# A hand-written order list for five engines, made longer and reordered at the start of a fused attention and channel-mix kernel

## The chip, the cores and the metric

The kernel runs on one core of one Trainium2 chip. The metric is the device time of one execution in microseconds (us); lower is better. Five engines take part: TensorE (PE, with its weight loads shown as PEld), VectorE (DVE), ScalarE (ACT), GpSimd (POOL), and SyncE (SP), which issues transfers.

## The reference

Two stages follow each other, in float32, for 4 sequences of 768 tokens and 512 features (8 heads of 64).

```python
for c in range(24):                       # chunks of 32 queries
    # keys: 8 memory rows and the window of up to 16 + 32 + 8 tokens around the chunk
    scores = 0.125 * q_c @ k_full.T
    a = exp(scores - max(scores)); a = a / (sum(a) + 1e-9)
    x[c] = a @ v_full
x_prev = x shifted by one token (zero in front)
xk = mu_k * x + (1 - mu_k) * x_prev
xr = mu_r * x + (1 - mu_r) * x_prev
k = maximum(xk @ w_k, 0)                  # 512 -> 1024
v = (k * k) @ w_v                         # 1024 -> 512
out = sigmoid(xr @ w_r) * v
```

## The kernel before

The 3072 tokens are dealt with in 12 units of 256 tokens, each of two tiles of 128. For unit u the work has these steps, and each is one named operation of a plan:

- `qk{t}` fetches the queries and keys of tile t, `vw{t}` its values. `s{u}` is the score product on PE (for unit 0 it is split: `s0` and `s0b`, one tile each). Then come `max{u}` and `sub{u}` on DVE, `exp{u}` on ACT, `sum{u}` on DVE, `norm{u}` on DVE or POOL.
- `t{t}` transposes the probabilities on PE (four products with the identity matrix `id`), `bd{t}.0` and `bd{t}.1` copy the two halves to SBUF on ACT or DVE, `a{t}` is the product with the values on PE, and `x{t}` copies the result out.
- For unit 0 alone the token shift is done on PE: `mix0.1` and `mix0.0` multiply the rows by two diagonal matrices, which `dg1` and `dg0` make from `id` and `mu` (lines 395 to 410). For later units `df{u}` and `mix{u}.m` do it on DVE. `xh{u}.m` and `xl{u}.m` split the result into a high and a low float32r part.
- `h{u}.n` is the product with w_k, `g{u}.n` that with w_r, `v{u}.n` that with w_v. Every one is made of three float32r products (high by high, high by low, low by high). `relu`, `sq`, `kh`, `kl` prepare the input of `v`; `sig` is the sigmoid, `o` the last multiplication, `out` the store.
- The weights come as ten loads of 1 MB, `w0.load` to `w9.load` (w0 and w1 are w_r, w2 to w5 are w_k, w6 to w9 are w_v). Each is decoded by `mag` (ACT), `low` and `join` (DVE), and split by `hi` and `lo`. `h0.0` needs w2 alone, `h0.1` w3, `h0.2` w4, `h0.3` w5. The `wz` operations form sums of w_v for a product scheme that later units use.

What decides the order is a planner (class `Plan`, lines 97 to 238). The list `FIRST` (lines 51 to 70) fixes order and engine of the first operations, up to `v0.3` in the kernel before; what is not in the list is placed greedily by due times, which `te_order` derives from `LEAD`. Every engine then works through its own instructions in that order. Transfers from HBM reuse four buffers named `big` (the `qk` and `w` loads), and a load waits until the buffer's last user is done.

Where the planner sees PE idle, the program adds "warm" products with a zero matrix (lines 1574 to 1580):

```python
n = 0 if ("ph", 0, 0) in T else int((o.start - busy - 0.1) / (0.86 if busy else 1.72))
```

Here `o.start` and `busy` are the planner's times, in which a `qk` load takes 1.68 of the transfer queue and lands 2.4 later, a `mu` load takes 0.1, a hop from engine to engine 0.17.

Of the kernel before, what the change touches and what calls it, by code (L numbers as in the profile page):

```python
# [50 lines left out]
FIRST = """
qk0@dma s0@pe qk1@dma max0@dve sub0@dve exp0@act s0b@pe max0b@dve mu@dma id@dma sum0@dve norm0@pool qk3@dma qk2@dma
w2.load@dma dg1@act vw0@dma vw1@dma w3.load@dma sub0b@dve exp0b@act sum0b@dve norm0b@dve dg0@act w2.mag@act s1@pe
t0@pe w4.load@dma bd0.0@act t1@pe w2.low@dve bd0.1@dve a0@pe w2.join@dve w2.hi@dve max1@dve sub1@dve qk5@dma
w2.lo@pool bd1.0@act bd1.1@act a1@pe qk4@dma x0@act x1@act mix0.0@pe mix0.1@pe w3.low@dve w3.mag@act w3.join@dve
vw2@dma exp1@act vw3@dma sum1@dve w5.load@dma w4.low@dve norm1@dve w4.mag@act w4.join@dve xh0.0@act w3.hi@act t2@pe
xl0.0@dve s2@pe xh0.1@act w4.hi@act bd2.0@act w0.load@dma bd2.1@dve w1.load@dma t3@pe bd3.1@act bd3.0@act a2@pe x2@act
xl0.1@dve w3.lo@dve qk6@dma a3@pe max2@dve h0.0@pe w4.lo@pool w5.mag@act w5.low@dve x3@act sub2@dve w5.join@dve
h0.1@pe h0.2@pe w0.low@dve vw4@dma exp2@act w0.mag@act sum2@dve w1.low@dve w5.hi@act w5.lo@dve h0.3@pe qk7@dma
w1.mag@act w0.join@dve w0.hi@act norm2@dve t4@pe w1.join@dve t5@pe w0.lo@dve relu0.1@act df1@dve relu0.0@act sq0.0@act  # L60
vw5@dma w1.hi@act bd5.1@act bd4.0@act w1.lo@dve sq0.1@act s3@pe g0.0@pe g0.1@pe relu0.2@act w7.load@dma mix1.1@dve
w6.load@dma mix1.0@dve bd4.1@act sq0.2@act kh0.1@act bd5.0@act xh1.1@dve xl1.1@dve w7.low@dve kl0.1@dve kh0.2@act
w8.load@dma xh1.0@act a4@pe xl1.0@dve kh0.0@act relu0.3@act kl0.0@dve w8.low@dve w7.mag@act w6.mag@act w9.load@dma
w7.join@dve w6.low@dve w6.join@dve sig0.0@act sig0.1@act a5@pe g1.0@pe g1.1@pe h1.0@pe sq0.3@act kh0.3@act h1.1@pe
kl0.3@pool x4@dve w7.hi@act x5@dve max3@dve sub3@dve sig1.0@act w7.lo@pool kl0.2@dve relu1.0@act sig1.1@act w6.hi@act
df2@dve w8.mag@act sq1.0@act w9.low@dve w6.lo@dve h1.2@pe h1.3@pe relu1.2@act relu1.1@act w9.mag@act relu1.3@act
sq1.2@act v0.0@pe w8.join@dve w9.join@dve sq1.3@act w8.hi@act mix2.1@dve v0.1@pe exp3@act w9.hi@act w8.lo@dve v0.2@pe
kh1.0@dve kl1.0@dve sq1.1@act w9.lo@dve kh1.1@act kl1.1@dve xh2.1@act xl2.1@dve mix2.0@dve kh1.2@act kl1.2@pool
v0.3@pe
"""  # L70
# [1560 lines left out]
```

## Time and profile before

| what | us |
|---|---|
| median of 3 runs | 390.93 (390.84 to 391.64) |
| the profiled execution | 391.39 |
| its span, first to last instruction | 389.6 |
| PE busy in the span | 381.5 |
| first product of mix0 starts | 19.30 |
| first product of g0.0 starts | 45.08 |

All times in the rows are microseconds from the start of the span, unless marked ns. A row of the timeline merges neighbouring instructions of one kind: start, length, engine, line of the kernel, operation, output and inputs, count, and in brackets how long the engine stood idle before it and what ended that.

### The profile page before, as it was taken

The page shows a single profiled execution, that of the slowest core. Times are in us where ns is not written, and L with a number is a line of the kernel's source. Part 1 is how long each engine was busy: PE and PEld are TensorE (multiplying, and loading weights), DVE is VectorE, ACT ScalarE, POOL GpSimd, SP SyncE. Part 2 cuts the span into 40 slices and gives each one's busy share as a digit, 9 for nine tenths or more (in the row PEclk, how much of TensorE's full clock was granted, in tenths as well). Part 3 has the DMA queues.
Part 4 walks back from the last instruction along what each step waited for, and adds up shares of the span by engine and source line. Part 5 has one row for each costly group of instructions (what it writes and reads, how often), then busy time and mean ns, then how long its engine had stood idle before and what let it go on. Part 6 is the DMA issues. An engine that isn't in the chain of part 4 may idle for free.

```text
span 389.6 us, 11005 instructions
## 1 busy us (share of the span) xinstructions
PE 381.5 (98%) x4736; PEld 351.8 (90%) x4736; DVE 324.2 (83%) x548; ACT 268.6 (69%) x455; POOL 16.0 (4%) x15
## 2 busy tenths in 40 slices
PE   8799999999999999999999999999999999999996
PEld 3589889888988999999999999999999899999996
DVE  3699999888898999969989989898999585976673
ACT  3877796914796789676588689877587746586631
POOL 2221004010000000000010000000000000000000
PEclk9999999999999999999999999999999999999999
DMA  8999870411053345435386576644046611133011
GB/s 314 414 374 368 324 301 2 141 56 54 2 204 116 130 154 183 153 128 216 116 309 211 193 272 207 216 175 144 2 163 190 203 56 42 32 132 109 0 56 54
DMA packets 25344, 63.43 MB, mean 163 GB/s; under 512 B 2512, under 2 KB 9040, under 8 KB 24784
## 3 DMA queue, kind: packets, MB, share of 16 engines
q1 hardware_dynamic: 25296, 62.73, 45.2%
q8 instruction: 37, 0.61, 0.7%
q14 instruction: 11, 0.09, 0.1%
HBM read 52.24 MB, written 10.49 MB: 161 GB/s over the span
## 4 chain that ended last, share of the span: by engine, by line
PE 92%; DMA 4%; ACT 2%; DVE 1%; SPq 0%; issue 0%
PE pr L1110 17%; PE ph L1134 15%; PE pc L1462 10%; PE pv L1110 9%; PE pa L1462 6%; PE B L1067 6%; PE pb L1462 6%; PE px L617 6%; PE G L1067 4%; PE A L1067 4%; PE s L520 4%; PE pt L600 2%; DMA vw<-in_vw_dram 2%; PE xf L671 2%; DMA wvl<-forms 1%; PE warm L1579 1%
## 5 line engine op out<-in xcount | busy, mean ns | idle before, releaser
L1134 PE MATMUL ph<-xh,wkh 128*128 128x256 f32 x192 | 53.5, 279 | 0.0
L1134 PE MATMUL ph<-xh,wkl 128*128 128x256 f32 x192 | 53.2, 277 | 0.1
L1134 PE MATMUL ph<-xl,wkh 128*128 128x256 f32 x192 | 53.1, 276 | 0.0
L1110 PE MATMUL pr<-wrh,xh 128*128 128x512 f32 x96 | 37.7, 393 | 0.0
L1110 PE MATMUL pr<-wrh,xl 128*128 128x512 f32 (+1 forms) x117 | 37.6, 351 | 0.0
L1110 PE MATMUL pr<-wrl,xh 128*128 128x512 f32 x96 | 37.5, 390 | 0.0
L1134 PEld LDWEIGHTS ph<-xh,wkl 128*128 128x128 f32 x192 | 36.0, 188 | 0.3 <-DVE wkl L448 0.3
L1134 PEld LDWEIGHTS ph<-xh,wkh 128*128 128x128 f32 x192 | 36.0, 188 | 0.3
L1409 DVE TENSOR_TENSOR khl<-k,khl 128x512 fp32r<-128x512 f32 x42 | 28.8, 688 | 8.8 <-ACT khl L375 8.3
L1134 PEld LDWEIGHTS ph<-xl,wkh 128*128 128x128 f32 x192 | 36.1, 188 | 0.0
L1110 PE MATMUL pv<-wvh,khl 128*128 128x512 f32 (+1 forms) x97 | 30.3, 390 | 0.0
L375 ACT CAST khl<-k 128x512 fp32r<-128x512 f32 x45 | 27.9, 621 | 2.6 <-PE pa L1462 1.5
L1462 PE MATMUL pc<-wtbig,khl 128*128 128x256 f32 x216 | 28.2, 280 | 0.0
L1462 PE MATMUL pa<-wvh,khl 128*128 128x256 f32 x144 | 28.2, 281 | 0.0
L375 ACT COPY aTz<-pt 64x512 f32<-64x512 f32 x43 | 24.8, 580 | 4.4 <-PE pt L600 3.6
L1462 PE MATMUL pb<-wtx,khl 128*128 128x256 f32 x216 | 27.5, 277 | 0.0
L617 PEld LDWEIGHTS px<-aTz,vw 128*64 128x64 f32 x768 | 23.5, 138 | 4.1 <-DVE aTz L377 2.3
L1229 ACT ACTIVATE k<-ph 128x512 f32<-128x512 f32 x23 | 13.5, 597 | 19.2 <-PE ph L1134 19.0
L617 PE MATMUL px<-aTz,vw 128*64 128x64 f32 x768 | 25.5, 224 | 1.2 <-DVE aTz L377 1.2
L1110 PEld LDWEIGHTS pr<-wrh,xl 128*128 128x128 f32 x117 | 22.0, 188 | 4.7
L1462 PEld LDWEIGHTS pc<-wtbig,khl 128*128 128x128 f32 x216 | 26.0, 188 | 0.1
L1462 PEld LDWEIGHTS pb<-wtx,khl 128*128 128x128 f32 x216 | 25.9, 188 | 0.0
(170 smaller groups left out, 1005.4 us busy)
## 6 DMA issues: line engine op xcount, KB each, us to landing
vw<-in_vw_dram SPq DMA_DIRECT2D x24, 512.0 KB, 5.0
ring<-in_qk_dram SPq DMA_DIRECT2D x16, 672.0 KB, 5.8
out_dram<-o SPq DMA_DIRECT2D x23, 256.0 KB, 2.2
qk<-in_qk_dram SPq DMA_DIRECT2D x8, 672.0 KB, 6.2
raw<-in_w_k_dram SPq DMA_DIRECT2D x4, 1024.0 KB, 7.7
raw<-in_w_v_dram SPq DMA_DIRECT2D x4, 1024.0 KB, 6.8
wvh<-forms SPq DMA_DIRECT2D x12, 256.0 KB, 3.4
wvl<-forms SPq DMA_DIRECT2D x12, 256.0 KB, 3.7
```

The lines of the kernel that those rows point to most:

```text
L375: e.copy(dst, src)
L520: nc.tensor.matmul(room(h, c)[CHUNK * j : CHUNK * (j + 1), r, :], q4[z, r, j, :], k3[z, r, STEP * j : STEP * j + NK], start=True, stop=True,)
L600: nc.tensor.transpose(p[:, n * P : (n + 1) * P], e[:, n // 2, c, n % 2, :], id_sb)
L617: nc.tensor.matmul(p3[64 * h : 64 * h + 64, 2 * g : 2 * g + 2, CHUNK * j : CHUNK * j + CHUNK], v[:, g, h, j, :], a[:, h, g, j, :], start=True,
L671: nc.tensor.matmul(z, T["diag", m][:, j, k], x[:, k, 1 - j : 1 - j + UTOK], start=j == 0, stop=j == 1)
L1067: nc.tensor.matmul(z, w, x[:, k], start=q in (1, 7) and i + k + m == 0, stop=i + k == 2 and m == 2, skip_group_check=q not in (1, 7),)
L1110: nc.tensor.matmul(p[:, a : a + step], x, w[:, a : a + step], start=start, stop=stop and a + step == DM)
L1134: nc.tensor.matmul(z, w, x[:, k], start=start, stop=stop)
L1229: e.activation(r, T["ph", u, f], AF.Relu)
L1409: nc.vector.tensor_sub(T["al", u, name], block(at), T["ah", u, name].bitcast(F32))
L1462: nc.tensor.matmul(p, l[:, i], r[i], start=start, stop=stop, skip_group_check=not fresh)
L1579: nc.tensor.matmul(warm, zero, zeros, start=True, stop=True)
```

## The change

The list is rewritten and goes on to `h2.3` and the first stores. VectorE makes the second diagonal matrix (`dg1`, two multiplications over 512 columns) in place of eight ScalarE activations; `1 - mu` becomes an operation of its own (`mu0`, `mu1`, ScalarE). The loads of `mu` and `id` are issued by ScalarE's queue and no longer by SyncE's. The warm products stop as soon as mix0 has begun, and no longer when h0 has begun.

```diff
-LEAD = """s0 t0 t1 a0 a1 mix0 mix1 h0.0 h0.1 s1 h0.2 h0.3 g0.0 g0.1 t2 t3 a2 a3
+LEAD = """s0 t0 t1 a0 a1 s1 mix0 mix1 h0.0 h0.1 h0.2 h0.3 g0.0 g0.1 t2 t3 a2 a3
...
-qk0@dma s0@pe qk1@dma max0@dve sub0@dve exp0@act s0b@pe max0b@dve mu@dma id@dma sum0@dve norm0@pool qk3@dma qk2@dma
-w2.load@dma dg1@act vw0@dma vw1@dma w3.load@dma sub0b@dve exp0b@act sum0b@dve norm0b@dve dg0@act w2.mag@act s1@pe
-t0@pe w4.load@dma bd0.0@act t1@pe w2.low@dve bd0.1@dve a0@pe w2.join@dve w2.hi@dve max1@dve sub1@dve qk5@dma
-w2.lo@pool bd1.0@act bd1.1@act a1@pe qk4@dma x0@act x1@act mix0.0@pe mix0.1@pe w3.low@dve w3.mag@act w3.join@dve
-vw2@dma exp1@act vw3@dma sum1@dve w5.load@dma w4.low@dve norm1@dve w4.mag@act w4.join@dve xh0.0@act w3.hi@act t2@pe
-xl0.0@dve s2@pe xh0.1@act w4.hi@act bd2.0@act w0.load@dma bd2.1@dve w1.load@dma t3@pe bd3.1@act bd3.0@act a2@pe x2@act
-xl0.1@dve w3.lo@dve qk6@dma a3@pe max2@dve h0.0@pe w4.lo@pool w5.mag@act w5.low@dve x3@act sub2@dve w5.join@dve
-h0.1@pe h0.2@pe w0.low@dve vw4@dma exp2@act w0.mag@act sum2@dve w1.low@dve w5.hi@act w5.lo@dve h0.3@pe qk7@dma
...
+qk0@dma s0@pe max0@dve mu@dma sub0@dve qk1@dma s0b@pe max0b@dve exp0@act qk2@dma sub0b@dve sum0@dve qk3@dma id@dma
+exp0b@act sum0b@dve norm0@dve w2.load@dma norm0b@pool mu1@act vw0@dma s1@pe max1@dve t0@pe mu0@act dg0@act bd0.0@act
+dg1@dve t1@pe vw1@dma w2.low@dve bd0.1@act bd1.0@act sub1@dve a0@pe x0@dve bd1.1@act w4.load@dma w2.mag@act w2.join@dve
+exp1@act w3.load@dma a1@pe sum1@dve w4.low@dve qk4@dma x1@act mix0.1@pe norm1@dve w2.hi@act qk5@dma w3.low@dve
+w4.mag@act w3.mag@act vw3@dma w4.join@dve w3.join@dve t2@pe mix0.0@pe bd2.0@act t3@pe xh0.1@act bd2.1@act w2.lo@dve
+vw2@dma w3.hi@act w3.lo@pool w5.load@dma xh0.0@act w4.hi@act bd3.0@act w5.mag@act xl0.1@dve bd3.1@act s2@pe xl0.0@dve
+w0.load@dma max2@dve w4.lo@pool sub2@dve a2@pe w0.mag@act w5.low@dve h0.0@pe w0.low@dve x2@act w5.join@dve exp2@act
+qk7@dma w1.load@dma a3@pe qk6@dma w0.join@dve sum2@dve w5.hi@act h0.1@pe w7.load@dma w0.hi@act w5.lo@dve w1.mag@act
+w1.low@dve h0.2@pe x3@act vw4@dma w1.join@dve w1.hi@act h0.3@pe s3@pe w9.load@dma norm2@dve t4@pe relu0.2@act w1.lo@dve
+w0.lo@dve df1@dve sq0.2@act t5@pe mix1.1@dve mix1.0@dve w9.low@dve relu0.0@act sq0.0@act relu0.3@act w6.load@dma
+vw5@dma xh1.0@dve w6.low@dve relu0.1@act bd5.1@act xl1.0@dve g0.0@pe bd4.0@act w7.mag@act bd5.0@act bd4.1@act
+w6.mag@act g0.1@pe kh0.0@act a4@pe w7.low@dve w8.load@dma w9.mag@act w6.join@dve sq0.3@pool max3@dve w8.low@dve
...
-    o_id = op("id", ("dma", 0.2), lambda: nc.sync.dma_start(id_sb, ident))
-    o_mu = op("mu", ("dma", 0.1), lambda: nc.sync.dma_start(mu_sb[:, 0:2], mu))
+    o_id = op("id", ("dma", 0.2), lambda: nc.scalar.dma_start(id_sb, ident))
+    o_mu = op("mu", ("dma", 0.1), lambda: nc.scalar.dma_start(mu_sb[:, 0:2], mu))
...
-            nc.scalar.activation(mu_sb[:, 2 + m], mu_sb[:, m], AF.Copy, scale=-1.0, bias=1.0)
             for j in range(2):
+                if m == 1:
+                    nc.vector.tensor_mul(
+                        T["diag", m][:, j],
+                        id_sb.unsqueeze(1).to_broadcast([P, KT, P]),
+                        mu_sb[:, m + 2 * j].unsqueeze(2).to_broadcast([P, KT, P]),
+                    )
+                    continue
...
-        diag[m] = (op(f"dg{m}", ("act", 2.0), f, [o_id, o_mu], new=d), d)
+        def f_rest():
+            nc.scalar.activation(mu_sb[:, 2 + m], mu_sb[:, m], AF.Copy, scale=-1.0, bias=1.0)
+
+        o = op(f"mu{m}", ("act", 0.2), f_rest, [o_mu])
+        diag[m] = (op(f"dg{m}", ("dve", 1.35, True) if m else ("act", 2.45), f, [o_id, o], new=d), d)
...
-                n = 0 if ("ph", 0, 0) in T else int((o.start - busy - 0.1) / (0.86 if busy else 1.72))
+                n = 0 if ("xf", 0, 0, 0) in T or ("xf", 0, 1, 0) in T else int((o.start - busy - 0.1) / (0.86 if busy else 1.72))
```

## Rows read from the trace of the kernel before

**Rows 1.** The page's first part: busy time of each engine, share of the span.

```profile
PE 381.5 (98%) x4736; PEld 351.8 (90%) x4736; DVE 324.2 (83%) x548; ACT 268.6 (69%) x455; POOL 16.0 (4%) x15
```

**Rows 2.** Timeline of PE, from s0b to the first mix0.

```profile
6.50 0.86 PE L520 MATMUL s<-qk 64*32 64x64 f32 x64 [0.69 <-DMA qk<-in_qk_dram]
7.29 2.84 PE L1579 MATMUL warm<-zero_sb 128*128 128x512 f32 x6
10.41 1.06 PE L520 MATMUL s<-qk 64*32 64x64 f32 x85 [0.28 <-DMA qk<-in_qk_dram]
12.62 0.68 PE L520 MATMUL s<-qk 64*32 64x64 f32 x43 [1.14 <-issue]
13.23 1.09 PE L600 MATMUL pt<-id_sb,e 128*128 128x128 f32 x8
...
16.00 2.09 PE L617 MATMUL px<-aTz,vw 128*64 128x64 f32 x64 [0.82 <-DVE aTz L377]
18.02 1.12 PE L1579 MATMUL warm<-zero_sb 128*128 128x512 f32 x2
19.30 7.14 PE L671 MATMUL xf<-xTs,k 128*128 128x256 f32 x32 [0.15 <-PE warm L1579]
```

**Rows 3.** The chain that ended last: start, length, what.

```profile
45.15 5.67 PE pr L1110 x25
...
386.41 0.42 DVE o L1501
```

**Rows 4.** Waits of PE over the span: total, times, longest.

```profile
PE px L617 <- DVE aTz L377: 1.2, 2, 0.8
```

**Rows 5.** The page's groups: busy, mean ns, idle before, releaser.

```profile
L1134 PEld LDWEIGHTS ph<-xh,wkl 128*128 128x128 f32 x192 | 36.0, 188 | 0.3 <-DVE wkl L448 0.3
```

**Rows 6.** Transfers issued from 10 to 11 us: instruction queue (packets, MB, share).

```profile
q8 instruction: 1, 0.02, 5.9%
```

**Rows 7.** Timeline of DVE up to 60 us.

```profile
12.46 0.69 DVE L559 TENSOR_TENSOR e<-e,sm_sb 128x512 f32<-128x512 f32 x1
...
26.84 1.28 DVE L685 TENSOR_TENSOR xl<-xf,xh 128x512 fp32r<-128x512 f32 x2
...
32.03 1.22 DVE L535 TENSOR_REDUCE sm_sb<-s 128x16 f32<-128x1024 f32 x1
33.18 0.68 DVE L438 TENSOR_SCALAR raw<-raw 128x1024 uint32<-128x1024 uint32 x1
33.77 1.22 DVE L544 TENSOR_TENSOR e<-s,sm_sb 128x1024 f32<-128x1024 f32 x1
34.91 1.22 DVE L442 SCALAR_TENSOR_TENSOR mag<-mag,raw 128x1024 uint32<-128x1024 uint32 x1
...
36.64 1.22 DVE L553 TENSOR_REDUCE sm_sb<-e 128x16 f32<-128x1024 f32 x1
...
38.27 0.64 DVE L438 TENSOR_SCALAR raw<-raw 128x1024 uint32<-128x1024 uint32 x1
...
58.05 2.22 DVE L442 SCALAR_TENSOR_TENSOR mag<-mag,raw 128x1024 uint32<-128x1024 uint32 x1
```

**Rows 8.** Timeline of ACT up to 22 us.

```profile
7.67 0.63 ACT L548 ACTIVATE e<-e 128x512 f32<-128x512 f32 x1 [5.65 <-DVE e L544]
...
11.26 2.43 ACT L405 ACTIVATE k<-id_sb,mu_sb 128x128 f32<-128x128 f32 x8
13.60 1.16 ACT L435 ACTIVATE xx<-raw 128x1024 f32<-128x1024 f32 x1
14.65 1.65 ACT L375 COPY aTz<-pt 64x512 f32<-64x512 f32 x3
...
20.58 1.06 ACT L548 ACTIVATE e<-e 128x1024 f32<-128x1024 f32 x1 [0.80 <-DVE e L544]
21.54 1.16 ACT L435 ACTIVATE mag<-raw 128x1024 f32<-128x1024 f32 x1
```

**Rows 9.** Transfers issued before 10 us: count, KB, us to landing.

```profile
id_sb<-in_ident_dram SPq DMA_DIRECT2D x1, 64.0 KB, 4.7
```

More of the change, by code (lines that the diff above doesn't have):

```diff
@@ L57 @@
-xl0.0@dve s2@pe xh0.1@act w4.hi@act bd2.0@act w0.load@dma bd2.1@dve w1.load@dma t3@pe bd3.1@act bd3.0@act a2@pe x2@act
-xl0.1@dve w3.lo@dve qk6@dma a3@pe max2@dve h0.0@pe w4.lo@pool w5.mag@act w5.low@dve x3@act sub2@dve w5.join@dve
-h0.1@pe h0.2@pe w0.low@dve vw4@dma exp2@act w0.mag@act sum2@dve w1.low@dve w5.hi@act w5.lo@dve h0.3@pe qk7@dma
-w1.mag@act w0.join@dve w0.hi@act norm2@dve t4@pe w1.join@dve t5@pe w0.lo@dve relu0.1@act df1@dve relu0.0@act sq0.0@act
-vw5@dma w1.hi@act bd5.1@act bd4.0@act w1.lo@dve sq0.1@act s3@pe g0.0@pe g0.1@pe relu0.2@act w7.load@dma mix1.1@dve
@@ L62 @@
[L62 to L66, printed above, removed]
@@ L67 @@
-sq1.2@act v0.0@pe w8.join@dve w9.join@dve sq1.3@act w8.hi@act mix2.1@dve v0.1@pe exp3@act w9.hi@act w8.lo@dve v0.2@pe
-kh1.0@dve kl1.0@dve sq1.1@act w9.lo@dve kh1.1@act kl1.1@dve xh2.1@act xl2.1@dve mix2.0@dve kh1.2@act kl1.2@pool
-v0.3@pe
+qk0@dma s0@pe max0@dve mu@dma sub0@dve qk1@dma s0b@pe max0b@dve exp0@act qk2@dma sub0b@dve sum0@dve qk3@dma id@dma
+exp0b@act sum0b@dve norm0@dve w2.load@dma norm0b@pool mu1@act vw0@dma s1@pe max1@dve t0@pe mu0@act dg0@act bd0.0@act
+dg1@dve t1@pe vw1@dma w2.low@dve bd0.1@act bd1.0@act sub1@dve a0@pe x0@dve bd1.1@act w4.load@dma w2.mag@act w2.join@dve
@@ new lines @@
+w1.low@dve h0.2@pe x3@act vw4@dma w1.join@dve w1.hi@act h0.3@pe s3@pe w9.load@dma norm2@dve t4@pe relu0.2@act w1.lo@dve
+w0.lo@dve df1@dve sq0.2@act t5@pe mix1.1@dve mix1.0@dve w9.low@dve relu0.0@act sq0.0@act relu0.3@act w6.load@dma
+vw5@dma xh1.0@dve w6.low@dve relu0.1@act bd5.1@act xl1.0@dve g0.0@pe bd4.0@act w7.mag@act bd5.0@act bd4.1@act
+w6.mag@act g0.1@pe kh0.0@act a4@pe w7.low@dve w8.load@dma w9.mag@act w6.join@dve sq0.3@pool max3@dve w8.low@dve
+xh1.1@act kh0.2@act kl0.0@dve xl1.1@dve kl0.2@dve w6.hi@act kh0.3@act w9.join@dve w8.mag@act w8.join@dve sq0.1@dve
@@ new lines @@
+a5@pe h1.0@pe relu1.0@act sig0.0@act w8.hi@act h1.1@pe w6.lo@dve w9.hi@act vw7@dma h1.2@pe qk8@dma sig0.1@act g1.0@pe
+wz0.01@dve w8.lo@dve w7.join@dve sq1.0@act kh0.1@act wz0.11@dve sig1.0@act wz0.t3@dve x4@act relu1.2@act kl0.1@dve
+w7.hi@act w9.lo@dve kl0.3@dve wz0.h3@act wz0.l3@dve h1.3@pe wz0.00@dve g1.1@pe w7.lo@pool x5@act sub3@dve relu1.1@act
+df2@dve v0.0@pe wz0.t1@dve sq1.2@act mix2.1@dve exp3@act v0.1@pe v0.2@pe v0.3@pe mix2.0@dve xh2.1@act wz0.10@dve
+relu1.3@act xh2.0@act wz0.t2@dve wz0.t4@dve xl2.0@dve wz0.h2@act wz0.l2@dve wz0.h1@act wz0.l1@dve h2.0@pe wz0.h4@act
@@ new lines @@
+wz0.l4@dve wz1.01@dve wz1.11@dve sig1.1@act xl2.1@dve wz1.t3@dve kh1.0@act wz1.h3@act sq1.1@act qk9@dma g2.0@pe
+sum3@dve o0.0@dve wz1.l3@dve g2.1@pe wz1.00@dve vw6@dma sq1.3@act o0.1@dve kh1.3@act kl1.0@dve kl1.3@dve wz1.t1@dve
+kh1.1@dve kl1.1@dve h2.1@pe wz1.h1@dve sig2.0@act kh1.2@dve wz1.t2@dve relu2.0@act wz1.h2@dve wz1.10@dve out0.0@dma
+wz1.t4@dve v1.0@pe kl1.2@pool wz1.l1@dve wz1.l2@dve sq2.0@act wz1.h4@dve norm3@dve v1.1@pe wz1.l4@dve sig2.1@act
+wz2.01@dve v1.2@pe wz2.11@dve wz2.t3@dve relu2.1@dve wz2.h3@dve sq2.1@dve wz2.l3@dve o1.0@dve v1.3@pe wz2.00@dve
@@ L70 @@
+wz2.t1@dve kh2.1@dve wz2.t2@dve h2.2@pe wz2.h1@dve kh2.0@dve out0.1@dma wz2.10@dve h2.3@pe wz2.t4@dve o1.1@dve
+out1.1@dma kl2.0@pool out1.0@dma
 """
```

## The prediction, made before the changed kernel ran

> **What bounds the kernel now.** The page's busy line comes first: PE 381.5 us of a 389.6 us span [rows 1]. The chain that ended last says where the rest is. It is PE from one end to the other, apart from the first 19 us, and closes with one DVE multiplication at 386.41 and its store [rows 3]. So only three things can move the time: when PE's unbroken work begins, the few holes in it, and what follows its last product. The change touches nothing of the last. PE's own list of waits is short: the attention product waits twice, 1.2 us in all [rows 4], of which 0.82 lie before mix0 [rows 2] and 0.4 before the next one. The page's group of h0's weight loads adds 0.3 us behind a DVE `lo` [rows 5].
>
> Now the timeline of PE. The first long work, mix0, starts at 19.30, and from there to g0.0 at 45.15 [rows 2, 3] PE needs 25.85 us, in which it stood for 0.4 (a2) and 0.3 (h0.3): 25.15 us without holes. After 45.15 the waits list has next to nothing left. The price of the whole change is thus read from two numbers, the start of mix0 and the holes up to g0.0. Before 19.30 PE holds little work, so what counts there is the chain of others: t0 and t1 at 13.23, ACT occupied by dg0 until 13.7 and by w2.mag until 14.65, only then the copies bd, a0 at 16.00, the x copies, and one superfluous pair of warm products that ends at 19.14 [rows 2, 8].
>
> The least obvious row is the one at 12.62. s1 stops after 85 of its 128 products and goes on 1.14 us later, with the cause "issue" [rows 2], that is nothing the profile shows. Just before, from 10 to 11 us, the instruction queue moved a packet of 0.02 MB [rows 6]. I read the hole as PE waiting for its next block of instructions.
>
> **The change part by part.**
>
> *Start to s1.* mu, now ahead of qk1 in the planner's order, moves the planned start of s0b by 0.1, so the gap that the warm formula sees grows from 0.81 to 0.91 and passes 0.86: one warm pair is put between s0 and s0b, and one fewer stands before s1. A pair is 2 of the 6 products of 2.84 us, 0.95 us, and s0b now starts at 6.50 after 0.69 us of idleness [rows 2], so it starts near 6.8, 0.3 us later. If the block of instructions is asked for while s0b runs, it too comes up to 0.3 us later. Bounds for the end of s1: 13.3 as before, 13.9 if the block is held up by twice that; I take 13.6, between them, since only one delay is in sight. As many instructions stand ahead of the hole as before, so by my reading it stays and the sum is the one below; if its cause were the time of a transfer, it could go, and the sum would be that of the first rival. Beside this: the Trainium skill, Runtime: NRT & Kernel Launch, § Terms, says that an engine's instruction memory is refilled in blocks of 16 KiB, so that a hole would be tied to a count of instructions. The packet's 0.02 MB agrees; no row names the engine that it served. The time that SP saves on mu and id brings qk2 and qk3 forward, but s1 runs into the hole anyway: worth nothing.
>
> *dg1 to VectorE, and what queues behind.* ACT loses eight activations, 2.43 us [rows 8], DVE gets two multiplications over 512 columns; the nearest row is the half norm, 0.69 [rows 7]. From below it is 0.6 each (overlapped, as the 0.68 `low` gives way after 0.59), from above 0.7: I take 1.3 for both. It isn't hidden: behind s1 DVE has max1, dg1, w2.low, sub1 in this order, ACT then exp1 and behind it x1, and mix0.1 waits for x1. From row starts: max1 1.15, dg1 1.3, low 0.6, sub1 its full 1.22, exp1 0.96 until the next ACT instruction starts, x1 0.59 (a 512-column copy like bd, 0.55 to 0.6) [rows 7, 8], and some 0.13 of hops. 13.6 + 1.15 + 1.3 + 0.6 + 1.22 + 0.96 + 0.59 + 0.13 = 19.55. The values don't bind: ACT, with dg0 (2.43) started after exp0b near 10, is free for bd0.0 when t0 is done near 14.2, four copies at 0.55 end by 16.4, and a0 and a1 are done by 17.5, before w2.mag and sub1 let exp1 begin at 17.9. So mix0 begins 0.25 us later than at present, between 19.2 and 19.9 with the bounds.
>
> *mix0 to g0.0.* PE's own work is the same 25.15 us if nothing is late. The check, from starts of rows [rows 7]: `low` 0.6, `sub` 1.14 (33.77 to 34.91) and so `join`, `lo` and `norm`, whose rows have the same length, `sum` 1.63 (36.64 to 38.27), two-part `xl` 1.28. norm1 ends 17.85 + x0 0.7 + 1.14 + 1.63 + 0.6 + 1.21 = 23.1, and t2 may start at 19.55 + 3.57 = 23.12: no slack. xl0.0, seven steps on, ends at 29.7, h0.0 is due at 30.2. w5.lo ends near 38.5, h0.3 is due at 39.5. In all DVE has 28 operations, 30 us, from max1 to w0.lo: 13.6 + 30.2 = 43.8, and g0.0 is due at 44.7. So the two old holes, 0.4 and 0.3, go: the second since w5.lo no longer stands behind w1.low, which waits for its load. w2.lo moves from POOL to DVE and w3.lo the other way, which cancels; w2.hi, bd0.1 and bd2.1 go to ACT (some 2.1 us less for DVE) and pay for dg1 and x0.
>
> *Rest of the list, LEAD and the condition on warm products.* No warm row stands behind 18.02 among those before h0, so the new condition removes none. The rest reorders a stretch in which PE had no hole; I cost it at nothing, under cover of PE's own work, and bound it by 0.3 of new waits (as rows 5) and 0 gain.
>
> Sum: mix0 +0.25, holes -0.7, 19.55 + 25.15 = 44.7 against 45.15: 0.45 us less. With the bounds of mix0 that is 0.1 to 0.8 less. The profiled execution took 391.39 (its span and 1.8 around it) and would take 390.9; the median of the runs lies 0.46 lower, so I say 390.5.
>
> **The rivals.** *The hole in s1 goes or ends early.* Then DVE goes from norm0 straight into max1. norm0 is done near 12.1, an estimate: the half norm at the end of the same chain ends at 13.15 now [rows 7], behind an exp0b that stood behind eight activations of 2.43 us on ACT [rows 8], and I take 1.1 of these off. max1 follows at once, and mix0 starts at 12.1 + 5.95 (the steps above) = 18.05: 19.3 - 18.05 and the 0.7 of holes make 1.95 us, 389.0. For it: the cause is inferred. Against: the count of instructions is equal.
>
> *DVE falls behind.* At t2 and at h0.0 the slack is 0 to 0.5, so each microsecond lost on DVE there is paid. The price is that of one `join` of 2.22 against 1.22 [rows 7], which ran beside POOL work: 1.0, which turns -0.45 into +0.55, 391.5. The list keeps POOL's work beside DVE's reads of PSUM, which speaks against it.
>
> *id comes late (slower).* On ScalarE's queue its load stands behind exp0 (7.67 to 8.30 now [rows 8]). If it is issued only then, and takes 0.8 to issue and 4.7 to land as now [rows 9], it lands at 13.8; dg0 ends at 16.2, four bd at 18.4, w2.mag 19.5, exp1 20.5, x1 21.1: mix0 at 21.1 and g0.0 at 46.3, 1.1 us slower, 392.0. It decides from a landing at 12.3 on, and is a loss from 12.7. Against it: nothing makes the transfer itself wait. Beside this: the Trainium skill, Perfetto Trace Analysis, § on DVE and Act instructions, has an engine's instruction wait in a queue of its own while the sequencer reads on; by that id goes out right after mu and the rival falls. No row here shows a transfer issued by ScalarE.
>
> **How the numbers follow.** A measurement of this kernel tells 0.2% (0.8 us) from no change. Forecast 0.48, of which 0.12 lies at its fast end beyond 0.8; no or short hole 0.25; small gains later 0.05 (faster); DVE behind 0.12 (same, or a little slower by 0.02); id late 0.10. Faster 0.42, same 0.46, slower 0.12. Range: from a little under the hole's absence, 388.8, to DVE behind, 391.5; outside lie the late id and a little at the fast end. The forecast's own range is 390.1 to 390.8.
>
> **What would show it.** Right: s1's second part near 12.9, dg1 on DVE between max1 and w2.low, x1 directly behind exp1 near 18.9, mix0.1 at 19.2 to 19.9, no wait at t2 or a2, g0.0 about 25.2 after mix0.1, the rest as before. Wrong: s1 without its hole; dg0 starting after 12; t2 or h0.0 waiting for DVE; new PE waits behind 45; a granted clock below 1.

## The result, and the profile of the changed kernel

The change made the kernel slower: 396.49 us (median of 6 runs, 395.73 to 397.27) against 390.91 (6 runs, 390.75 to 392.58), a ratio of 1.0134, 95% interval 1.0111 to 1.0157. The forecast was 390.5. The profiled execution took 397.19, 5.80 more than that of before.

First the two numbers to which the forecast had reduced everything, the start of mix0 and what follows it. In the timeline of PE of the changed kernel (`warm` are the filling products, `pt` belongs to t0 and t1, `px` to a0 and a1, `xf` to mix0):

```profile
5.44 1.18 PE L537 MATMUL s<-qk 64*32 64x64 f32 x64 [0.59 <-DMA qk<-in_qk_dram]
6.55 1.13 PE L1596 MATMUL warm<-zero_sb 128*128 128x512 f32 x2
7.61 0.86 PE L537 MATMUL s<-qk 64*32 64x64 f32 x64
8.39 1.98 PE L1596 MATMUL warm<-zero_sb 128*128 128x512 f32 x4
10.31 1.07 PE L537 MATMUL s<-qk 64*32 64x64 f32 x85
14.53 0.92 PE L537 MATMUL s<-qk 64*32 64x64 f32 x43 [3.16 <-issue]
15.60 1.94 PE L617 MATMUL pt<-id_sb,e 128*128 128x128 f32 x8
19.06 3.69 PE L634 MATMUL px<-aTz,vw 128*64 128x64 f32 x64 [1.52 <-ACT aTz L382]
22.68 1.58 PE L1596 MATMUL warm<-zero_sb 128*128 128x512 f32 x2
24.36 3.69 PE L688 MATMUL xf<-xTs,k 128*128 128x256 f32 x16
```

mix0 starts at 24.36 instead of 19.30 [rows 2], 5.06 us later. From there to the end of the span it is 395.4 - 24.36 = 371.0 us against 389.6 - 19.30 = 370.3 before. So 5.06 of the 5.8 us are lost ahead of mix0 and 0.7 behind it. Ahead of it, three things differ from rows 2. The hole in s1 (the stretch with the cause "issue") is 3.16 us long instead of 1.14. a0 starts 3.06 later. And the products of a0 and a1 need 3.69 for what took 2.09.

The timeline of ACT says why a0 is late (`ACTq` is ACT's queue issuing a transfer):

```profile
0.75 0.40 ACTq L399 DMA_DIRECT2D mu_sb<-in_mu_dram  x1
1.18 1.28 ACT L565 ACT_TABLE_LOAD   x1 [1.18 <-PEq L1636]
8.48 0.63 ACT L565 ACTIVATE e<-e 128x512 f32<-128x512 f32 x1 [6.02 <-DVE e L561]
8.49 0.36 ACTq L398 DMA_DIRECT2D id_sb<-in_ident_dram  x1
...
15.49 2.45 ACT L418 ACTIVATE k<-id_sb,mu_sb 128x128 f32<-128x128 f32 x8 [4.73 <-DMA id_sb<-in_ident_dram]
17.84 1.77 ACT L382 COPY aTz<-pt 64x512 f32<-64x512 f32 x3
```

mu goes out at once. id does not: its issue appears at 8.49, 0.01 behind the start of exp0, which stands ahead of it on ACT and waits for DVE until 8.48. Then the transfer takes 7.0 us to land, where SyncE's took 4.7 [rows 9]:

```profile
id_sb<-in_ident_dram ACTq DMA_DIRECT2D x1, 64.0 KB, 7.0
```

ACT stands idle for 4.73 us, dg0 starts at 15.49, and bd0.0, on which a0 waits, is queued behind dg0 on ACT. The chain of work that ended last runs through this load and not through s1 (start, length, what; the longest pieces):

```profile
8.49 6.97 DMA id_sb<-in_ident_dram
19.06 3.70 PE px L634 x64
24.36 3.69 PE xf L688 x16
```

Why a0 and a1 are slow shows in the windows (per stretch: span, busy time and instructions of PE, PEld, DVE, ACT, POOL, granted clock, DMA share, GB/s), first of the changed kernel, then of before:

```profile
10.00:13.00 3.00, 1.38 (x86) 0.91 (x85) 2.35 (x7) 0.76 (x3) 0.89 (x1) 1.00 0.99 406
13.39:23.63 10.24, 7.43 (x116) 6.25 (x117) 6.71 (x8) 7.68 (x17) 0.00 (x1) 0.50 0.79 322
23.63:30.00 6.37, 6.27 (x30) 5.01 (x29) 6.30 (x9) 4.22 (x6) 0.00 (x0) 1.00 0.88 304
```

```profile
13.39:23.63 10.24, 9.26 (x96) 7.06 (x96) 8.73 (x9) 8.37 (x15) 2.37 (x1) 1.00 1.02 413
```

From 13.39 to 23.63 TensorE was granted half its clock, 1.2 GHz of 2.4. The fall came in s1's hole, 2.0 us after its last product and 2.1 us before id landed. In the kernel before, the clock was whole throughout the span.

### The profile page after: what moved, and what is told of

Its sections match the earlier page's. It is cut to its first block, busy times and chain, and to the rows that moved or that the text cites. A ratio compares the mean times of both kernels' runs of the same rounds, so it can differ in the third digit from the quotient of the medians.

```text
span 395.4 us, 11007 instructions
## 1 busy us (share of the span) xinstructions
PE 384.8 (97%) x4734; PEld 354.8 (90%) x4734; DVE 327.0 (83%) x556; ACT 264.9 (67%) x441; POOL 16.5 (4%) x16
## 4 chain that ended last, share of the span: by engine, by line
PE 91%; DMA 6%; ACT 1%; DVE 1%; SPq 0%; issue 0%
PE ph L1151 17%; PE pr L1127 15%; PE pc L1479 10%; PE pv L1127 8%; PE px L634 6%; PE pa L1479 6%; PE B L1084 6%; PE pb L1479 6%; PE G L1084 4%; PE A L1084 4%; PE s L537 4%; PE pt L617 2%; DMA vw<-in_vw_dram 2%; PE xf L688 2%; DMA id_sb<-in_ident_dram 2%; DMA wvl<-forms 1%
## 5 line engine op out<-in xcount | busy, mean ns | idle before, releaser
L382 ACT COPY aTz<-pt 64x512 f32<-64x512 f32 x46 | 26.7, 580 | 6.1 <-PE pt L617 5.3
L634 PE MATMUL px<-aTz,vw 128*64 128x64 f32 x768 | 27.5, 232 | 2.2 <-ACT aTz L382 1.5
L634 PEld LDWEIGHTS px<-aTz,vw 128*64 128x64 f32 x768 | 25.2, 145 | 4.7 <-ACT aTz L382 1.9
L382 ACT CAST khl<-k 128x512 fp32r<-128x512 f32 x41 | 25.4, 622 | 2.0 <-PE pa L1479 0.9
L1198 ACT ACTIVATE sg<-pr 128x512 f32<-128x512 f32 x24 | 14.4, 599 | 17.4 <-PE pr L1127 15.8
```

The costliest lines, as they stand in the source:

```text
L382: e.copy(dst, src)
L634: nc.tensor.matmul(p3[64 * h : 64 * h + 64, 2 * g : 2 * g + 2, CHUNK * j : CHUNK * j + CHUNK], v[:, g, h, j, :], a[:, h, g, j, :], start=True,
L1198: nc.scalar.activation(T["sg", u][:, c * DM : (c + 1) * DM], T["pr", u, c], AF.Sigmoid)
```

## The experiments

All times of rows come from each kernel's profiled execution. "Rest" is its span less the start of mix0, so it grows by every wait and every slower product behind mix0. Two kernels ran once only and have no ratio. Each ratio compares with runs of before made beside that kernel's own; their medians lie between 390.91 and 391.94.

| kernel | median us | ratio to before, 95% | id lands | s1 resumes | mix0 | rest |
|---|---|---|---|---|---|---|
| before | 390.91 | | 6.8 | 12.62 | 19.30 | 370.3 |
| after | 396.49 | 1.0134 (1.0111 to 1.0157) | 15.5 | 14.53 | 24.36 | 371.0 |
| E1 after, both loads on SyncE | 394.90 | 1.0087 (1.0058 to 1.0115) | 11.3 | 13.67 | 20.30 | 371.8 |
| E2 after, id ahead of exp0 | 394.88 | 1.0081 (1.0065 to 1.0097) | 7.3 | 13.68 | 20.32 | 372.2 |
| E3 before, both loads on ScalarE | 399.39 | 1.0207 (1.0182 to 1.0233) | 16.0 | 12.76 | 27.17 | 370.3 |
| E4 before, no warm ahead of s1 | 393.48 | single run | 7.5 | 13.09 | 21.01 | 370.7 |
| E5 after, no pair ahead of s0b | 397.70 | 1.0155 (1.0127 to 1.0183) | 15.0 | 13.19 | 23.24 | 372.3 |
| E6 as E1, list mended | 396.89 | 1.0127 (1.0100 to 1.0154) | 11.8 | 14.51 | 20.63 | 375.2 |
| E7 before, two more switches | 392.63 | single run | 7.1 | 13.00 | 19.30 | 371.6 |
| E8 before, dg1 on VectorE | 391.82 | 1.0009 (0.9996 to 1.0022) | 7.0 | 12.78 | 19.59 | 370.2 |
| E9 start of before, rest of after | 396.02 | 1.0126 (1.0096 to 1.0156) | 7.1 | 13.33 | 19.52 | 374.0 |
| E10 start of after, rest of before | 393.67 | 1.0047 (1.0030 to 1.0064) | 7.1 | 12.62 | 19.26 | 372.3 |
| E11 after, loads in the old order | 393.47 | 1.0053 (1.0030 to 1.0075) | 6.9 | 12.98 | 19.61 | 374.8 |
| E12 before, mix0 earlier | 395.30 | 1.0082 (1.0058 to 1.0106) | 7.0 | 12.62 | 17.54 | 376.2 |
| E13 as E12, t2 in time | 395.19 | 1.0077 (1.0057 to 1.0096) | 7.0 | 12.99 | 17.56 | 375.5 |
| E14 as E11, three moves | 395.95 | 1.0108 (1.0073 to 1.0143) | 6.9 | 13.13 | 19.76 | 374.2 |

(id lands = issue plus time to landing. E11's profiled execution was its slowest, 396.23, 2.8 above its median; its rest is that of this execution.)

**E1 and E2: id early, by two ways.**

```diff
 E1
-    o_id = op("id", ("dma", 0.2), lambda: nc.scalar.dma_start(id_sb, ident))
-    o_mu = op("mu", ("dma", 0.1), lambda: nc.scalar.dma_start(mu_sb[:, 0:2], mu))
+    o_id = op("id", ("dma", 0.2), lambda: nc.sync.dma_start(id_sb, ident))
+    o_mu = op("mu", ("dma", 0.1), lambda: nc.sync.dma_start(mu_sb[:, 0:2], mu))
 E2
-qk0@dma s0@pe max0@dve mu@dma sub0@dve qk1@dma s0b@pe max0b@dve exp0@act qk2@dma sub0b@dve sum0@dve qk3@dma id@dma
+qk0@dma s0@pe max0@dve mu@dma id@dma sub0@dve qk1@dma s0b@pe max0b@dve exp0@act qk2@dma sub0b@dve sum0@dve qk3@dma
```

> The changed kernel with the loads of mu and id issued by SyncE again, in the places that the new list gives them (id behind the four qk loads). Theory (the identity matrix is late on ScalarE's queue): id lands near 11 in place of 15.49, the diagonal on ScalarE starts at once, mix0 starts near 19.5 to 20.5 in place of 24.36, and most of the 5.6 us comes back: 390.5 to 392. Rival (the new order, with s1's hole and the fallen clock, costs the time by itself): the hole stays near 3 us, the clock falls, 394 to 396.5.

> The changed kernel with id still on ScalarE's queue, but ahead of exp0 in the list. Theory (id was late because its issue stood behind exp0, which waits for the first scores): id is issued near 1.2 and lands by 6, and the result is as with SyncE's queue, 390.5 to 392. Rival (a load on the second queue is slow whenever it is issued, since SyncE's loads fill the transfer engines): id lands after 9 and mix0 stays after 21.

Both give 4.1 us of the start of mix0 back and keep the whole clock; their times, 394.9, do not reach the 390.5 to 392 of their theories. In E2 the queue is the same ScalarE queue; only the place in the list differs:

```profile
1.18 0.46 ACTq L398 DMA_DIRECT2D id_sb<-in_ident_dram  x1
10.20 2.43 ACT L418 ACTIVATE k<-id_sb,mu_sb 128x128 f32<-128x128 f32 x8
```

The transfer's place behind exp0 is thus the cause, not the queue. PE of E1:

```profile
13.67 0.68 PE L537 MATMUL s<-qk 64*32 64x64 f32 x43 [2.13 <-issue]
...
16.21 2.45 PE L634 MATMUL px<-aTz,vw 128*64 128x64 f32 x64 [0.84 <-ACT aTz L382]
...
20.30 3.72 PE L688 MATMUL xf<-xTs,k 128*128 128x256 f32 x16 [0.59 <-DVE xx L459]
```

From E1 the 5.06 us split: id on time leaves 1.0 (20.30 - 19.30), and 4.06 go with the late id. Of these, 2.85 lie ahead of a0 (19.06 against 16.21 in E1) and 1.21 between a0 and mix0, at the half clock. Two things came back together with id: s1 resumes 0.86 earlier in E1 than in the changed kernel, and the clock stays whole. That the half clock is id's doing is not shown, since it began in the hole, before the first product that needs id. With id on time mix0 follows the end of s1 by 5.95 to 5.96 us in the five kernels that keep the new steps up to mix0 (E1, E2, E10, E11, E14; in E1 from 14.35 to 20.30), so there s1's end sets it. s1's end at 15.45 in the changed kernel would by this give 21.40, and the 2.96 from there to 24.36 are what the late id, with the half clock behind it, cost on top of the hole as it was. 0.8 to 0.9% of loss stay in both.

**E3: the late loads in the kernel before.** Only the two loads move to ScalarE's queue, where that list has them behind exp0.

```diff
-    o_id = op("id", ("dma", 0.2), lambda: nc.sync.dma_start(id_sb, ident))
+    o_id = op("id", ("dma", 0.2), lambda: nc.scalar.dma_start(id_sb, ident))
...
```

> The kernel before with only the two loads moved to ScalarE's queue; its list has both behind exp0. Theory (queue): mu and id are issued near 8 and land near 14 to 15, the first diagonal waits, exp0b stands behind it on ScalarE, t1 and all behind it come later: mix0 near 23 to 25, 394.5 to 397. Rival (the loads matter only with the new order): 390.9 to 392.

The same mechanism in the old list costs more than the whole change, and more than its theory said: mix0 at 27.17, and the rest is the 370.3 of before. The clock was half here too, from 13.81 to 24.05. Timeline of ACT:

```profile
7.89 0.63 ACT L548 ACTIVATE e<-e 128x512 f32<-128x512 f32 x1 [5.86 <-DVE e L544]
7.90 0.38 ACTq L392 DMA_DIRECT2D mu_sb<-in_mu_dram  x1
8.31 0.45 ACTq L391 DMA_DIRECT2D id_sb<-in_ident_dram  x1
14.56 0.20 ACT L402 ACTIVATE mu_sb<-mu_sb 128x4 f32<-128x4 f32 x1 [6.04 <-DMA mu_sb<-in_mu_dram]
```

Here dg1 stands ahead of exp0b on ACT, so the second half of the softmax waits for id too.

**E4 and E5: the hole in s1 and the clock.**

```diff
 E4 (before)
-                n = 0 if ("ph", 0, 0) in T else int((o.start - busy - 0.1) / (0.86 if busy else 1.72))
+                n = 0 if ("ph", 0, 0) in T or o.name == "s1" else int((o.start - busy - 0.1) / (0.86 if busy else 1.72))
 E5 (after)
-                n = 0 if ("xf", 0, 0, 0) in T or ("xf", 0, 1, 0) in T else int((o.start - busy - 0.1) / (0.86 if busy else 1.72))
+                n = 0 if o.name == "s0b" or ("xf", 0, 0, 0) in T or ("xf", 0, 1, 0) in T else int((o.start - busy - 0.1) / (0.86 if busy else 1.72))
```

> The kernel before without the six warm products between s0b and s1. Theory (s1's hole is a wait for instructions, and falls at a count of them): the hole comes six products later, after 91 of s1's 128. Rival (it is tied to a moment or to a transfer): it stays after 85 or goes. On the clock: if PE's work ahead of 13 us keeps it up, it falls to half in this run; if not, it stays at 1.0 and the time is that of the kernel before, 391.

> The changed kernel without the pair of warm products that the new list puts between s0 and s0b; id stays on ScalarE's queue behind exp0. Theory (the length of s1's hole hangs on when s0b runs, and the fall of the clock on the length of the hole; the late id is a cost of its own): s0b starts about 0.7 earlier, the hole ends near 12.8 to 13.5, the clock stays at 1.0, id still lands near 15, and mix0 starts at 21.5 to 22.5: 393.5 to 395, so 2 us of the 5.6 are the clock's. Rival (the clock falls because PE waits for id): hole shorter, but the clock still falls by 14, 395.5 to 396.5.

PE of E4 with the stretch of its half clock, then PE of E5:

```profile
10.83 1.56 PE L520 MATMUL s<-qk 64*32 64x64 f32 x91 [2.61 <-DMA qk<-in_qk_dram]
13.09 0.87 PE L520 MATMUL s<-qk 64*32 64x64 f32 x37 [0.69 <-issue]
...
7.78:18.02 10.24, 6.93 (x178) 4.80 (x166) 7.39 (x16) 8.87 (x25) 1.04 (x1) 0.50 1.01 412
```

```profile
9.59 1.09 PE L537 MATMUL s<-qk 64*32 64x64 f32 x87
13.19 0.66 PE L537 MATMUL s<-qk 64*32 64x64 f32 x41 [2.50 <-issue]
15.12 1.94 PE L617 MATMUL pt<-id_sb,e 128*128 128x128 f32 x8 [1.27 <-DVE sm_sb L552]
```

With six products fewer ahead of it the hole comes after 91 products instead of 85, with two fewer after 87. Counted from the start of the program it comes after 223 products in fourteen of the 16 profiles, and after 222 in E12 and E13, where t0 stands ahead of s1: its place is a count of instructions. The Trainium skill (Runtime: NRT & Kernel Launch, § Terms) has an engine's instruction memory refilled in blocks of 16 KiB; the runs agree.

The end of the hole is not set by the count. The packet of 0.02 MB on the instruction queue [rows 6] shows what ends it: in all 16 profiles TensorE goes on 2.2 to 2.5 us behind the start of such a packet (10.39 and 12.62 before, 12.07 and 14.53 after, 11.41 and 13.68 in E2). No row names the engine that the packet serves, but the distance hardly varies, so the hole is read as a wait for instructions on their way. What sets the start of the packet is open. s1 resumes 5.9 to 6.9 us behind the start of s0b, but s0b alone does not set it: in E1 s0b started 0.13 later than in the changed kernel (7.74 against 7.61), and s1 went on 0.86 earlier.

E5 also shows that the length of the hole alone does not lower the clock. The hole is 0.66 shorter than after's, and the half clock came all the same, as the rival said, from 14.91 to 21.74, in the wait ahead of t0 that follows the hole; E2, with a hole of 2.77 but id at 7.3, kept the whole clock. E5's earlier mix0 (23.24) earned nothing, since its rest grew to 372.3.

E4 does not show what the six warm products are worth. Its clock fell at 7.78, while s0b ran and before the place from which they were taken; in this run qk0 had come late, s0 started at 5.51 instead of 4.77, and TensorE had stood for 0.84 and 0.86. The stand of 2.61 came after the fall. Its rest is 370.7, and mix0 lies 1.7 later; how much of this is the edit's stays open, with a single run.

**E6: four moves that were to mend E1.** Beside E1's and E5's edits:

```diff
-dg1@dve t1@pe vw1@dma w2.low@dve bd0.1@act bd1.0@act sub1@dve a0@pe x0@dve bd1.1@act w4.load@dma w2.mag@act w2.join@dve
-exp1@act w3.load@dma a1@pe sum1@dve w4.low@dve qk4@dma x1@act mix0.1@pe norm1@dve w2.hi@act qk5@dma w3.low@dve
+dg1@dve t1@pe vw1@dma w2.low@dve bd0.1@act bd1.0@act a0@pe x0@dve sub1@dve bd1.1@act w4.load@dma w2.mag@act w2.join@dve
+a1@pe x1@act exp1@act w3.load@dma sum1@dve w4.low@dve qk4@dma mix0.1@pe norm1@dve w2.hi@act qk5@dma w3.low@dve
...  bd3.1 ahead of w5.mag; vw5's load ahead of w6's
```

> The changed kernel with both loads on SyncE's queue, without the warm pair ahead of s0b, with x0 ahead of sub1 and x1 ahead of exp1, bd3.1 ahead of w5.mag (which waits for its load) and the vw5 load ahead of w6's. Theory (what the run with both loads on SyncE's queue still loses is the hole of 2.1, x1 behind exp1, a3 behind w5.mag, a5 behind vw5, and some 0.8 for more changes of kind on PE): mix0 near 18.5 to 19, both later waits of the attention product gone, 391 to 392. Rival (DVE sets the pace from s1 to g0 whatever stands ahead): mix0 early, but new waits of t2 or h0 for DVE, 393 to 395.

Neither came out. qk1, issued in one go with the other two qk loads as in E1, landed only when s0b started, at 8.31 (7.74 in E1), the clock was half from 8.24 to 11.65, and the wait that vw5 had caused moved to the next: w6's load, now behind vw5's, kept VectorE idle, and h1.0 waited 2.56 for `xl`.

**E7 and E8: two prices in the kernel before.** E7 alternates g1 and h1, E8 makes dg1 on VectorE in a stretch in which VectorE was idle.

```diff
 E7
-w7.join@dve w6.low@dve w6.join@dve sig0.0@act sig0.1@act a5@pe g1.0@pe g1.1@pe h1.0@pe sq0.3@act kh0.3@act h1.1@pe
+w7.join@dve w6.low@dve w6.join@dve sig0.0@act sig0.1@act a5@pe g1.0@pe h1.0@pe g1.1@pe sq0.3@act kh0.3@act h1.1@pe
 E8
-w2.load@dma dg1@act vw0@dma vw1@dma w3.load@dma sub0b@dve exp0b@act sum0b@dve norm0b@dve dg0@act w2.mag@act s1@pe
+w2.load@dma vw0@dma vw1@dma w3.load@dma sub0b@dve mu1@act dg1@dve exp0b@act sum0b@dve norm0b@dve mu0@act dg0@act w2.mag@act s1@pe
```

> The kernel before with g1.0, h1.0, g1.1, h1.1 on PE in place of g1.0, g1.1, h1.0, h1.1: two more changes between kinds of product, all else as it was. Theory (each change of kind costs PE 0.1 to 0.2): from the start of g1 to the end of h1 PE needs 16.7 to 16.9 us in place of 16.5, with no wait. Rival (the pieces cost nothing, and the lost time of the changed kernel between mix0 and v1 is all waits): 16.5.

> The kernel before with only the second diagonal made by VectorE, in the idle stretch that it has while exp0b runs, and 1 - mu as operations of their own. Theory (dg1 costs DVE 1.3, hidden there; ScalarE comes free 2.4 earlier but then waits for w2's load, and PE waits for the hole): mix0 within 0.3 of 19.3, 390.5 to 391.7. Rival (dg1 on DVE delays the chain of DVE by its length): mix0 near 20.5, 392.3 or more.

E7's g1 and h1 took 16.59 us from their first product to the first of v0, against 16.48 in before, E3, E4, E8 and E10 alike: 0.06 for each of the two more switches, less than the 0.1 to 0.2 of its theory. (Its other 1.5 us are a wait for the load `wvl` at 304, up to 1.0 in other runs.) From mix0 on the changed list changes the kind of product 164 times, the old one 156, so the estimate by E7 is 8 x 0.06 = 0.5 us. The groups of products agree in direction (before, then after; busy, mean ns, idle):

```profile
L1134 PE MATMUL ph<-xh,wkh 128*128 128x256 f32 x192 | 53.5, 279 | 0.0
...
L617 PE MATMUL px<-aTz,vw 128*64 128x64 f32 x768 | 25.5, 224 | 1.2 <-DVE aTz L377 1.2
```

```profile
L1151 PE MATMUL ph<-xh,wkh 128*128 128x256 f32 x192 | 53.9, 281 | 0.0
...
L634 PE MATMUL px<-aTz,vw 128*64 128x64 f32 x768 | 27.5, 232 | 2.2 <-ACT aTz L382 1.5 <-DMA vw<-in_vw_dram 0.6
```

(px needs 26.1 in E1, E2 and E11, which have the whole clock there; so 1.4 of its 2.0 are the half clock's.) E8 is no different from before: the move of dg1 into an idle stretch is worth nothing either way.

**E9, E10, E11: the two lists crossed at mix0, and the loads in the old order.** mu and id are on SyncE in all three, with SyncE's order qk0, qk1, mu, id, qk3, qk2.

```diff
 E10 and E11, order of the loads
-qk0@dma s0@pe max0@dve mu@dma sub0@dve qk1@dma s0b@pe max0b@dve exp0@act qk2@dma sub0b@dve sum0@dve qk3@dma id@dma
+qk0@dma s0@pe max0@dve qk1@dma sub0@dve mu@dma s0b@pe max0b@dve exp0@act id@dma sub0b@dve sum0@dve qk3@dma qk2@dma
 E9: E8's list up to mix0.1, then the new list; E10: the new one up to mix0.1, then E8's, with the old LEAD
```

> The list of the kernel before up to its two mix0 products (with dg1 on VectorE in an idle stretch, which cost nothing measurable, and mu and id on SyncE), and from there on the list of the changed kernel. Theory: of the 3.4 us that stay when id comes early, about 2 lie behind mix0, in the new list (products of different kinds alternate more often, and single waits at a3 and a5 of 0.6 to 1.3): mix0 at 19.3 to 19.7, 392.3 to 393.5. Rival: the new list behind mix0 is as good as the old one and all of the loss is in the start: 390.7 to 391.5.

> The list of the changed kernel up to its first mix0 product, with mu and id on SyncE and the loads in the order of before (qk0, qk1, mu, id, qk3, qk2; so without the warm pair ahead of s0b), and from there on the list of the kernel before. Theory: the start costs little by itself once id, mu and qk1 come in the old order: s0b at 6.5, hole until 12.6, mix0 at 19.4 to 20.0, 391.0 to 391.8. Rival: the start is what costs (dg1 behind max1 on VectorE, exp1 ahead of x1): mix0 past 20.3, 392.3 and more.

> The changed kernel with mu and id on SyncE and the loads of its start in the order of before (qk0, qk1, mu, id, qk3, qk2), all else new. If the losses of the start and of the rest simply add: mix0 at 19.4 to 20.0 and about 2 us lost behind it, 392.5 to 393.7, that is 1.2 to 2.4 less than with the two loads alone put back (394.9). Rival: the order of the qk loads is worth nothing, 394.5 to 395.2.

The old order of the loads also takes away the warm pair ahead of s0b. mix0 starts at 19.26 to 19.61 in all three, within 0.31 of before, and all three are slower than before. So what is left lies behind mix0. E9, the new list behind the old start, lost 1.3%, more than its theory said; E10 lost 0.5%: its mix0 came slightly earlier than its theory said and its time was the rival's, by the old list's waits for VectorE behind the new start; E11 was the expected sum at its median. The waits of PE, of E9 and of E10:

```profile
PE px L634 <- DMA vw<-in_vw_dram: 1.2, 1, 1.2
...
PE ph L1151 <- ACT xh L382: 0.5, 1, 0.5
...
PE px L634 <- ACT aTz L382: 0.4, 1, 0.4
PE pr L1127 <- DVE wrl L465: 0.4, 1, 0.4
```

```profile
PE px L627 <- DVE aTz L377: 1.4, 1, 1.4
...
PE pt L610 <- DVE e L569: 0.7, 1, 0.7
```

Every row is a small lateness of VectorE, ScalarE or a load. In the changed kernel itself nearly none of them shows (the rest is 371.0): mix0 came 5 us late there, and the others had caught up meanwhile. The one that stays is a5's for vw5, whose load was issued only at 49.54, behind w6's, and took 7.73 to land:

```profile
57.31 1.15 PE L634 MATMUL px<-aTz,vw 128*64 128x64 f32 x32 [0.64 <-DMA vw<-in_vw_dram]
```

**E14: three moves for the waits that are left.** Beside E11's list:

```diff
 bd3.1@act ahead of w5.mag@act; vw5@dma ahead of w9.load@dma; h1.3@pe ahead of g1.0@pe
```

> As e11 (changed list, loads in the old order) with three moves for what stood open behind mix0: bd3.1 ahead of w5.mag on ScalarE, vw5's load ahead of w9's on the transfer queue, and h1.3 ahead of g1.0 on TensorE. Theory: the rest of the loss is single waits (a3 1.12, a5 1.66 in e11) and the alternation of h and g: the waits at a3 and a5 go, the w_k products take some 0.2 less, 391.8 to 392.8. Rival: the waits only move to the next operation behind VectorE or the loads, 393.2 to 394.5.

The rival's mechanism held; the time, 395.95, lies above its 393.2 to 394.5. The waits at a3 and a5 are gone, and in their place stand one of 1.23 at a w_k product (55.42, for `xl`) and one of 0.69 at a w_r product (70.24). The w_k products took no less than in E11. As in E6, taking single waits away moved them on.

**E12 and E13: an earlier mix0 in the kernel before.**

```diff
-w2.load@dma dg1@act vw0@dma vw1@dma w3.load@dma sub0b@dve exp0b@act sum0b@dve norm0b@dve dg0@act w2.mag@act s1@pe
-t0@pe w4.load@dma bd0.0@act t1@pe w2.low@dve bd0.1@dve a0@pe w2.join@dve w2.hi@dve max1@dve sub1@dve qk5@dma
-w2.lo@pool bd1.0@act bd1.1@act a1@pe qk4@dma x0@act x1@act mix0.0@pe mix0.1@pe w3.low@dve w3.mag@act w3.join@dve
+vw0@dma vw1@dma w2.load@dma w3.load@dma sub0b@dve mu1@act dg1@dve exp0b@act sum0b@dve norm0b@dve mu0@act dg0@act t0@pe
+s1@pe w4.load@dma bd0.0@act bd0.1@dve t1@pe bd1.0@act bd1.1@dve a0@pe max1@dve sub1@dve a1@pe x0@act x1@act w2.low@dve
+w2.mag@act w2.join@dve exp1@act qk5@dma w2.hi@dve w2.lo@pool qk4@dma mix0.0@pe mix0.1@pe w3.low@dve w3.mag@act
...
 E13 beside this
+w2.mag@act exp1@act w2.join@dve qk5@dma sum1@dve qk4@dma mix0.0@pe mix0.1@pe norm1@dve w2.hi@act w3.mag@act w3.low@dve
...
```

> The kernel before with a shorter way to mix0: dg1 on VectorE ahead of exp0b, vw0 and vw1 loaded ahead of w2, t0 ahead of s1 on TensorE (so that the hole, which comes after a count of instructions, stands beside softmax work), the copies of t0 and t1 ahead of w2's decoding, max1 and sub1 ahead of it too, no warm products behind s1, and w5's lo ahead of w1.low. Theory: mix0 starts at 16.8 to 17.5 instead of 19.30; VectorE and the weight loads then become late at h0 or g0, which gives part of it back: 389.2 to 390.4. Rival: the weights' arrival sets g0.0 whatever the start is, 390.7 to 391.3; or the granted clock falls in the stretch without warm products and it is slower, 392 to 394.

> As e12 (mix0 at 17.54 there, but t2 waited 3.54 us for norm1, because VectorE took two joins, one of them 3.21 us beside GpSimd's lo, ahead of sum1), with sum1 and norm1 ahead of w3's decoding, w2's hi on ScalarE, w2's lo on VectorE behind norm1, and w4's low and join behind xl0.0. Theory: the gain of the start is kept where VectorE serves the softmax before the weights: mix0 at 17.5, t2 without a wait, the granted clock full, and of the 1.8 us some 0.8 to 1.8 are left at the end: 389.2 to 390.6. Rival: the weights become late instead (h0.1 to h0.3 or g0.0 wait for VectorE): 390.8 to 392.5.

mix0 came 1.75 us earlier, about as worked out, and both kernels were 0.8% slower, past the ranges of theory and rival alike. PE of E12, then of E13:

```profile
17.54 7.17 PE L681 MATMUL xf<-xTs,k 128*128 128x256 f32 x32 [0.69 <-ACT xTs L375]
28.25 1.09 PE L610 MATMUL pt<-id_sb,e 128*128 128x128 f32 x4 [3.54 <-DVE e L569]
29.27 1.75 PE L530 MATMUL s<-qk 64*32 64x64 f32 x102
31.89 0.66 PE L530 MATMUL s<-qk 64*32 64x64 f32 x26 [0.87 <-issue]
```

```profile
17.56 7.17 PE L681 MATMUL xf<-xTs,k 128*128 128x256 f32 x32 [0.69 <-ACT xTs L375]
24.57 0.60 PE L610 MATMUL pt<-id_sb,e 128*128 128x128 f32 x4
25.10 1.22 PE L530 MATMUL s<-qk 64*32 64x64 f32 x102
28.49 0.66 PE L530 MATMUL s<-qk 64*32 64x64 f32 x26 [2.17 <-issue]
```

In E12 t2 waited 3.54 for norm1: VectorE's `join` at 21.60 took 3.21 beside POOL's `lo`. In E13 t2 came in time, as its theory said, but a second hole of instructions, again after 102 products of s2, took 2.17, and h0 waited 0.85 for the low part of a weight. Here too TensorE went on 2.3 (E12) and 2.45 us (E13) behind the start of a packet on the instruction queue. From the end of either long wait the granted clock was half, 28.11 to 34.93 and 28.52 to 31.93. No version beat the kernel before.

## Why the prediction was wrong

**id on ScalarE's queue.** This is the step that failed: the sum took id to be there when dg0 wanted it, near 10, and put its wait at nothing. It landed at 15.5, and mix0 came at 24.36 and not at 19.55. The late id had been written down as a rival with 0.10 (392.0). It was judged too unlikely, by "nothing makes the transfer itself wait", and beside that stood the Trainium skill's rule (Perfetto Trace Analysis, § DVE / Act Engine Instruction), that the sequencer reads on while an instruction waits. In three traces id or mu did not pass the waiting instruction: it was issued 0.01 us behind the start of exp0, which had waited 5.5 to 6 us (after, E3, E5), and in E2, listed ahead of exp0, at 1.18. The rival was also priced too low. It took 4.7 from issue to landing, from a row of another queue at an emptier time; 7.0 were measured, so 15.5 and not 13.8. With the rival's own chain mix0 would start at 21.1 + 1.7 = 22.8. The remaining 1.6 stand behind a1: x1 waited 0.38 for it and was done at 23.38, and the pair of warm products that stands ahead of mix0 on PE ended at 24.26. a0 and a1 (3.69, in E1 2.45) and this pair (1.58, in E1 1.12) ran at the half clock, which the prediction named only as something that would make it wrong.

**The hole in s1.** Its cause, a block of instructions, was right (E4, E5 and the packets), and that the pair moved s0b was too. The size was off: s0b came at 7.61, not 6.8, since s0 itself started at 5.44 against 4.77 before and the pair ran behind it, and s1 resumed at 14.53, not 12.9. The bound of 13.9 for s1's end was passed by 1.55. s0 waited for qk0; it started at 5.22 to 5.44 in the three profiles in which ScalarE issues mu at 0.75 (after, E2, E5) and at 4.77 to 4.89 in the others, but for E4 with 5.51, so that mu's move delays qk0 is likely and not shown. Costing the new order of the loads at "worth nothing" belongs here: from E1 to E11, with qk1, mu and id back in their old order and the warm pair gone, s1 resumes 0.7 and mix0 starts 0.7 earlier, and the ratio falls from 1.0087 to 1.0053 (the intervals overlap).

**The rest of the list at nothing, bounded by 0.3.** In the changed kernel it cost 0.7. Against it stand 0.6 for a5's new wait, whose cause lies in the order of the loads, and some 0.5 by E7 for more switches, less 0.7 for the two old holes, which did go as forecast; that makes 0.4, and 0.3 stay open. In the shadow of a mix0 5 us late this was cheap. With mix0 at 19.5 to 19.6 the same list cost 3.7 in the profile of E9 (374.0) and 1.8 in E11, if its median is taken (393.47 less 1.8 around the span, less 19.61, is 372.1). The slack worked out at t2, h0.0 and g0.0 was VectorE's alone, and only up to 45. In E9 three waits, 1.3 in all, lie ahead of 45, at a2 and h0.0, and two of them are for ScalarE; two more, 0.4 and 1.2, lie behind it, the longer one for a load.

**What held.** The sum of the steps from s1's end to mix0, 5.95, came out in E1, E2, E10, E11 and E14, where id is in time (5.95 to 5.96). dg1's multiplications took 1.28 us, forecast 1.3, and made in an idle stretch they cost nothing (E8). (g0.0 was read from the chain, at 45.15; its first product starts at 45.08, which changes nothing.) That the end follows from mix0's start plus a constant held for the old list, in five profiles with mix0 between 19.3 and 27.2: the rest is 370.2 to 370.7 in before, E3, E4 and E8, and 371.6 in E7 with its 1.5 at 304. It does not hold for an earlier mix0 (E12, E13) nor for the new list.

Open: of E11's 0.5%, how much is switches and how much waits that vary from run to run; E14 took two of these waits away and was slower. Open too: what delays the packet that ends s1's hole, and what lowered the clock in the changed kernel and not in E2.
